# Spreading attention units over the stages of a fused attention and expert kernel: 12, 10, 8, 10, 5 in place of 10, 10, 10, 8, 7

## The chip, the cores and the metric

The kernel runs on one core of a Trainium2 chip. The metric is the device time of one execution in microseconds, the median of several runs. Before the change it is 318.38 us (three runs, 317.75 to 319.08). The profiled execution spans 316.5 us; the times of single instructions below are read in it, counted from its start.

## What is computed

Sliding-window attention with a distance bias, for 8 batches of 8 heads, 576 positions and 64 values per head, feeds an expert layer with 512 inputs, 2048 hidden values and 512 outputs per token. Inputs and output are float32.

```python
scores = (1.0 / np.sqrt(D)) * np.matmul(q, k.transpose(0, 1, 3, 2))
bias = slopes[:, None, None] * (-np.abs(rel))[None, :, :]
mask = (rel >= 0) & (rel < 128)
scores = np.where(mask, scores + bias[None], -1e9)
attn = softmax(scores)                       # over the last axis
x = np.matmul(attn, v).transpose(0, 2, 1, 3).reshape(B * S, H * D)
h = x @ w_in
g = h * np.cos(h)
out = g @ w_out
```

## The kernel before

The tokens, 4608 in all, pass through the expert layer in nine chunks of 512. Attention works in 72 units: for each batch eight units of a pair of heads and a half (256 queries), and a tail unit for the last 64 queries of all heads. Units are done in a fixed order, the first nine ahead of chunk 0, and the rest in stages: stage c stands between the first expert layer of chunk c and that of chunk c + 1, beside the second layer of chunk c. `QUOTA` says how many units each stage takes.

```python
QUOTA = [9, 9, 10, 10, 10, 8, 7]
...
def units(b):
    return [(b, pr, G) for G in range(2) for pr in range(NPAIR)] + [(b, "t", None)]
...
every = [u for b in range(B) for u in units(b)]
attention(every[0:9], -1)
done = 9
next_t = 2
for c in range(NCH):
    if c == 0:
        ...                                   # first layer of chunk 0, in halves
    else:
        for fc in range(NFC):
            moe1(c, fc, ...)                  # first layer, cosine, product
    n = QUOTA[c] if c < len(QUOTA) else 0
    attention(every[done:done + n], c)
    done += n
    while next_t < B and done >= 9 * (next_t - 1):
        load_v(next_t)
        if next_t < 4:
            tail_zero(next_t)
        dma_transposes(next_t)                # q and k of this batch, by SyncE's queue
        next_t += 1
        if next_t < B:
            load_nat("q", q, next_t)          # natural q, k, by GpSimd's queue
            load_nat("k", k, next_t)
    moe2(c)                                   # second layer
```

A stage's units go in groups of two. A group with a tail does its two value products one after the other. A finished unit has to be turned, from tokens along partitions to features along partitions. How this is done depends on when the next layer needs it: by DMA if the chunk of its first token is beyond the next stage's, and otherwise by TensorE with a copy by ScalarE or VectorE.

```python
def attention(us, phase):
    for g in range(0, len(us), 2):
        two = us[g:g + 2]
        ...                                   # scores, exponentials, masks
        for set_ in sets:
            pv(set_)                          # values
            after = []
            for u, ub in set_:
                n = ucount[0]
                ucount[0] += 1
                norm(u, ub, n)                # reciprocal and product, into xnat
                first = (S * u[0] + (512 if u[1] == "t" else 256 * u[2])) // CH
                after.append((first > phase + 1, u, ub, n))
            for by_dma, u, ub, n in after:
                if by_dma:
                    x_dma(u, n)
                else:
                    x_pe(u, ub, n)

def x_pe(u, ub, n):                           # two 128x128 transposes, then a copy
    ...
            for r in range(2):
                ins = e.transpose(dst[:, 128 * r:128 * r + 128],
                                  xnat[n % NX][:, 128 * r:128 * r + 128], ident[:, :])
    ...
    op(("act", "dve"), {"act": lambda e: e.activation(o, i, ACTF.Copy),
                        "dve": lambda e: e.tensor_copy(o, i)}, ...)

def x_dma(u, n):                              # one DMA transpose on SyncE's queue
    ...
    op("sp", [lambda e: e.dma_start_transpose(
        xT[:, pr, t0:t0 + 256].rearrange("p (r t) -> p r t", r=2), xnat[n % NX][:, :])], ...)
```

The order of instructions on each engine is not written by hand. The kernel records operations with their tiles, and a list scheduler with a model of durations, run when the kernel is built, places them: each engine takes the operation that can start soonest, by priority among those close together. GpSimd's operations keep the order in which they are recorded. ScalarE alternates between the exponential and the sine, stage by stage. SyncE's queue carries the transposes of q and k, the transposes of finished units and the stores of the output. The scores of batch b read buffers that batch b + 2 uses again, so a transpose of q or k waits for the last scores two batches before.

The second layer sums 16 matmuls per 128 tokens, the first layer four per 128 hidden values; both stream 512 columns per matmul.

Of the kernel before, what the change touches and what calls it, by code (L numbers as in the profile page):

```python
# [250 lines left out]
def bass_alibi_sliding__then__act_gcu_kernel(  # L251
# [8 lines left out]
    with ExitStack() as ctx:  # L260
# [31 lines left out]

        ps = ctx.enter_context(nc.psum_tensor("ps", [128, 8, 512], F32))
        BPE = 2
        QUOTA = [9, 9, 10, 10, 10, 8, 7]
        SB, UB, OB = [4, 5, 6, 7], [2, 3], [0, 1]

        slopes = [2.0 ** (-8.0 * (h + 1) / H) for h in range(H)]
# [487 lines left out]
# [4 lines that stand above are left out]
                if phase < 0:  # L790
                    for n, u in enumerate(two):
                        scores([u], n)
                        exps(u, n, 0)
                        mask(u)
                else:
                    scores(two, 0)
                    for n, u in enumerate(two):
                        exps(u, n, 2 * phase + 2)
                    for u in two:
                        mask(u)  # L800
                sets = [list(zip(two, OB if phase < 0 and g == 0 else UB))]
                if any(u[1] == "t" for u in two):
                    sets = [[s] for s in sets[0]]
                for set_ in sets:
                    pv(set_)
# [4 lines that stand above are left out]
                        norm(u, ub, n)  # L810
# [7 lines that stand above are left out]
# [27 lines left out]
        for c in range(NCH):  # L845
# [8 lines left out]
            else:  # L854
                for fc in range(NFC):
                    moe1(c, fc, (UB + SB)[fc % 6] if done < len(every) else
                         (UB + SB)[(16 * c + fc) % 6])
            n = QUOTA[c] if c < len(QUOTA) else 0
            attention(every[done:done + n], c)
# [40 lines left out]
```

The softmax here doesn't subtract the row's maximum and nothing guards it: scores larger than these inputs give would overflow.

## Time and profile before

| | before |
|---|---|
| median time | 318.38 us |
| span of the profiled execution | 316.5 us |
| matmuls on TensorE | 2480 |
| busy share of TensorE, ScalarE, VectorE, GpSimd | 96%, 66%, 60%, 30% |
| bytes moved by DMA | 37.63 MB |
| transposes of finished units by TensorE (line 661) | 80, for 40 units |
| DMA transposes of finished units (line 684) | 24 |

In the page's slices a digit is the busy share of one fortieth of the span (7.9 us), in tenths. A group's row gives the line, the engine, the operation, output and inputs, shape and count, then busy time, mean duration of one in ns and the idle time ahead of it. Durations of matmuls are modelled and overlap; the step from one start to the next tells what a matmul takes of TensorE. A timeline row has the start, the length, the engine, the line, the operation, its tiles and the count. A row of waits says who waited for whom, with the total in us, the number of times and the longest. "Landing" of a transfer is counted from its issue. Line 507 is scores, 498 scores of a tail, 592 and 595 values, 579 and 581 values of a tail, 697 the first layer, 768 the second, 742 the second layer's last tile; lines 372 and 375 are the DMA transposes of q and k (512 positions, then 64).

### The profile page before, as it was taken

Reading aid. Unit: us, or ns where it says so; the run is one execution under the profiler, and the core shown is the slowest. Engines: PE = TensorE matmul, PEld = TensorE weight load, DVE = VectorE, ACT = ScalarE, POOL = GpSimd, SP = SyncE. Lnnn points to the kernel's source line nnn. Section 1 sums busy time; section 2 is a strip of 40 time slices with the busy share of each in tenths; the row PEclk is TensorE's granted clock in tenths of the full one; section 3 lists DMA queues with packets and bytes.
Section 4 is the critical chain, followed back from the end, with each engine's and each line's share of the span. In section 5 each row is a group of like instructions: output and inputs, shape, how many; then the busy total and the mean of one; then the engine's idle time right before and its main releaser. Section 6 shows DMA issues by size and latency. Waiting matters only on the chain.

```text
span 316.5 us, 6268 instructions
## 1 busy us (share of the span) xinstructions
PE 304.9 (96%) x2480; PEld 155.9 (49%) x2480; DVE 188.5 (60%) x448; ACT 209.5 (66%) x306; POOL 95.1 (30%) x122
## 2 busy tenths in 40 slices
PE   2899999999999999999999999999999999999996
PEld 2677755444544544445444544544455444444444
DVE  3798757867685735848785878586555461363000
ACT  6896877886798746878687767857675553362211
POOL 8997140099946325701941300000000000000000
PEclk9999999999999999999999999999999999999999
DMA  7999999999999999999999894320012001201112
GB/s 139 178 207 208 206 164 186 142 139 190 140 131 173 174 151 203 156 142 132 150 165 143 112 143 77 106 68 18 25 74 47 33 0 48 87 0 68 66 72 94
DMA packets 142604, 37.63 MB, mean 119 GB/s; under 512 B 132208, under 2 KB 137328, under 8 KB 142576
## 3 DMA queue, kind: packets, MB, share of 16 engines
q0 software_dynamic: 99344, 18.10, 76.3%
q1 hardware_dynamic: 43232, 19.15, 31.9%
q8 instruction: 19, 0.31, 0.4%
q14 instruction: 9, 0.07, 0.1%
HBM read 36.70 MB, written 9.44 MB: 146 GB/s over the span
## 4 chain that ended last, share of the span: by engine, by line
PE 62%; DMA 18%; POOL 11%; SPq 6%; issue 1%; ACT 0%; POOLq 0%; ACTq 0%
PE ps L768 28%; PE ps L697 26%; DMA qnat<-in_q_dram 14%; SPq L372 6%; POOL vp L351 4%; POOL qnat L361 3%; PE ps L507 2%; DMA qt<-qnat 2%; DMA kt<-knat 2%; PE ps L592 2%; POOL knat L361 1%; PE ps L742 1%; POOL w_outb L389 1%; PE ps L595 1%; POOL w_inb L383 1%
## 5 line engine op out<-in xcount | busy, mean ns | idle before, releaser
L768 PE MATMUL ps<-w_outb,gT 128*128 128x512 bf16 x560 | 135.1, 379 | 0.0
L697 PE MATMUL ps<-xT,w_inb 128*128 128x512 bf16 x512 | 115.8, 379 | 0.0
L706 DVE TENSOR_TENSOR gT<-ps,cos 128x512 bf16<-128x512 f32 x128 | 81.9, 686 | 42.2 <-PE ps L768 29.8
L702 ACT ACTIVATE cos<-ps,halfpi 128x512 f32<-128x512 f32 x128 | 81.6, 688 | 29.2 <-PE ps L697 16.1
L768 PEld LDWEIGHTS ps<-w_outb,gT 128*128 128x128 bf16 x560 | 51.1, 98 | 54.7 <-issue 2.1
L697 PEld LDWEIGHTS ps<-xT,w_inb 128*128 128x128 bf16 x512 | 48.6, 98 | 57.5 <-DVE gT L706 4.0
L537 ACT ACTIVATE p<-ps 128x768 bf16<-128x768 f32 (+1 forms) x64 | 55.3, 915 | 15.4 <-PE ps L507 13.5
L351 POOL DMA_DIRECT2D vp<-in_v_dram x40 | 33.9, 890 | 58.1 <-PE ps L595 37.8
L561 DVE TENSOR_TENSOR p<-p,emask 128x512 bf16<-128x512 bf16 (+1 forms) x96 | 40.8, 461 | 14.9 <-ACT p L537 14.4
L774 ACT ACTIVATE ob<-ps 128x512 f32<-128x512 f32 x28 | 16.8, 599 | 41.8 <-PE ps L768 41.7
L361 POOL DMA_DIRECT2D qnat<-in_q_dram x30 | 25.6, 910 | 25.8 <-DMA qt<-qnat 18.4
L361 POOL DMA_DIRECT2D knat<-in_k_dram x30 | 25.6, 928 | 2.2 <-PE ps L720 2.2
L633 DVE TENSOR_TENSOR xnat<-ps,rec 128x256 bf16<-128x256 f32 x64 | 24.4, 420 | 0.3
L507 PE MATMUL ps<-qt,kt 64*128 64x128 bf16 (+1 forms) x320 | 19.1, 245 | 1.5 <-DVE kt L470 0.9
L592 PEld LDWEIGHTS ps<-vp,p 128*128 128x128 bf16 x256 | 15.5, 98 | 7.9 <-issue 4.3
L592 PE MATMUL ps<-vp,p 128*128 128x65 bf16 x256 | 18.3, 194 | 0.4 <-DVE p L561 0.2
L507 PEld LDWEIGHTS ps<-qt,kt 64*128 64x128 bf16 x320 | 11.4, 96 | 12.5 <-ACT p L537 4.0
L631 DVE RECIPROCAL rec<-ps 128x4 f32<-128x4 f32 x64 | 8.2, 167 | 15.5 <-PE ps L595 15.1
L595 PE MATMUL ps<-vp,p 128*128 128x65 bf16 x192 | 17.1, 193 | 0.0
L720 PE MATMUL ps<-xT,w_inb 128*128 128x256 bf16 x128 | 16.4, 273 | 0.2
L670 ACT ACTIVATE xT<-ps 128x256 bf16<-128x256 bf16 x27 | 9.9, 387 | 6.6 <-PE ps L661 6.5
L595 PEld LDWEIGHTS ps<-vp,p 128*128 128x128 bf16 x192 | 13.4, 97 | 0.4
(54 smaller groups left out, 174.6 us busy)
## 6 DMA issues: line engine op xcount, KB each, us to landing
out_dram<-ob SPq DMA_DIRECT2D x35, 256.0 KB, 2.3
vp<-in_v_dram POOLq DMA_DIRECT2D x32, 128.0 KB, 11.3
qnat<-in_q_dram POOLq DMA_DIRECT2D x24, 128.0 KB, 12.4
knat<-in_k_dram POOLq DMA_DIRECT2D x24, 128.0 KB, 15.7
w_inb<-in_moe_w_in_dram POOLq DMA_DIRECT2D x4, 512.0 KB, 10.7
w_outb<-in_moe_w_out_dram POOLq DMA_DIRECT2D x4, 512.0 KB, 22.5
qrows<-in_q_dram POOLq DMA_DIRECT2D x1, 576.0 KB, 15.4
krows<-in_k_dram POOLq DMA_DIRECT2D x1, 576.0 KB, 17.5
```

The costliest lines, as they stand in the source:

```text
L351: op("pool", [lambda e, t=t, rows=rows: e.dma_start(vp[b % 2][0:rows, t, :, 0:64], v[b, :, 128 * t:128 * t + rows, :].rearrange("h p d -> ...
L361: fns.append(lambda e, t=t, rows=rows: e.dma_start(nat[which][b % 2][0:rows, t, :, :], src[b, :, 128 * t:128 * t + rows, :].rearrange("h p ...
L507: ins = e.matmul(ps[:, banks[x], c0:c1], keys_ap(b, x, pr, kc), query_ap(b, x, pr, qb, 128 * nb), start=True, stop=True)
L537: op("act", lambda e: e.activation(P[i][:, :, 0:hi], src_[:, :, 0:hi], ACTF.Exp, scale=0.125), w=held + [("P", i)], occ=920 if G else 691, ...
L561: op("dve", lambda e, p=p, m=m: e.tensor_tensor(p, p, m, ALU.mult), r=[("P", i), ("EM", h0), ("EM", h1)], w=[("P", i)] if n != 1 else [("P ...
L592: ins = e.matmul(o, P[i][:, x, d0:d0 + 128], V[:, kc, h, 0:65], start=True, stop=not two)
L595: ins = e.matmul(o, P[i][:, x, p0:p0 + 128], V[:, kc - 1, h, 0:65], start=False, stop=True)
L633: op("dve", lambda e: e.tensor_tensor(o, U[:, :, :, 0:64], rv[:, :, :, None].broadcast_to([128, 2, 2, 64]), ALU.mult), r=[("rec", n % 2)], ...
L697: op("pe", lambda e, kc=kc: e.matmul(ps[:, bank, :], w_in[:, kc, 128 * fc:128 * fc + 128], xT[:, kc, r0:r0 + CH], start=(kc == 0), stop=(k ...
L702: op("act", lambda e: e.activation(cosb[ci][:, :], ps[:, bank, :], ACTF.Sin, bias=halfpi[:, 0:1]), r=["halfpi"], w=[("B", bank), ("cos", c ...
L706: op("dve", lambda e: e.tensor_tensor(gT[gi][:, fc, :], ps[:, bank, :], cosb[ci][:, :], ALU.mult), r=[("cos", ci)], w=[("B", bank), ("g", ...
L768: op("pe", lambda e, t=t, fc=fc, bank=bank: e.matmul(ps[:, bank, :], gT[gi][:, fc, 128 * t:128 * t + 128], w_out[:, fc, :], start=(fc == 0 ...
```

## The change

Five numbers of `QUOTA` change, of which one (10 units in stage 3) comes out the same. Two units move from stage 3's start to stage 2's end, two from stage 4 to stage 3, and two from stage 6 to stage 5. The numbers of instructions of attention and of the expert layers stay, as do thresholds, buffers and priorities; how a unit is turned follows from the rule above, and the scheduler lays out anew what comes after. Its purpose is a distribution of attention work over the stages that the schedule's model, in which DMA engines are shared between the queues, finds shorter. The other items that the change is named after (the first q piece by SyncE's queue, a block of w_in ahead of the rest of V, doubled natural q and k tiles) are in the kernel before already.

```diff
         BPE = 2
-        QUOTA = [9, 9, 10, 10, 10, 8, 7]
+        QUOTA = [9, 9, 12, 10, 8, 10, 5]
         SB, UB, OB = [4, 5, 6, 7], [2, 3], [0, 1]
```

## The prediction

> **What bounds the kernel now.** I read four views of the profile of before, from the coarse to the fine. First the page: the busy line, the slices and the two costliest groups.
>
> ```profile
> PE 304.9 (96%) x2480; PEld 155.9 (49%) x2480; DVE 188.5 (60%) x448; ACT 209.5 (66%) x306; POOL 95.1 (30%) x122
> ...
> PE   2899999999999999999999999999999999999996
> ...
> DMA  7999999999999999999999894320012001201112
> ...
> L768 PE MATMUL ps<-w_outb,gT 128*128 128x512 bf16 x560 | 135.1, 379 | 0.0
> L697 PE MATMUL ps<-xT,w_inb 128*128 128x512 bf16 x512 | 115.8, 379 | 0.0
> ```
>
> TensorE is at 9 tenths in every slice but the first two and the last. The 379 ns of a matmul is a modelled, pipelined time and does not add up (1072 of 379 ns would be 406 us), so a busy PE row does not yet prove that PE is the bound. What proves it is start to start: in the timeline near the end 48 matmuls stand between 299.82 and 310.18, so one takes 10.36/48 = 0.216 us, and the stretches inside attention keep the same pace. Second view, TensorE's waits from 118 us to the end, which is where the change acts:
>
> ```profile
> PE ps L498 <- DMA kt<-knat: 0.6, 1, 0.6
> ```
>
> That is the whole answer. In 198 us TensorE has one visible wait, 0.6 us, for the key transpose of batch 4. Third, the chain that ended last: from that wait on it is TensorE's own instructions, back to back, except for the closing copy of ScalarE.
>
> ```profile
> 112.00 6.59 DMA kt<-knat
> 118.58 0.05 issue
> 118.63 0.41 PE ps L498 x16
> 119.04 0.17 PE ps L507 x4
> 119.20 1.40 PE ps L768 x6
> ```
>
> So before 118.6 us the chain goes through DMA (18% of the span), and after it time can fall only if TensorE has fewer instructions, or cheaper changes between kinds. It can rise by any new wait. ScalarE (66%) and VectorE (60%) are not the bound in the mean; the DMA engines are at 9 tenths until about 190 us, so what needs a transfer there can be late.
>
> **What the Trainium skill says.** *Perfetto Trace Analysis*, section "Identifying the Most-Contended Engine", says that matmul busy time is no good measure of closeness to the roofline; this trace agrees (379 ns shown, 0.216 us start to start), so I count starts. *TensorE: Matmul & The Clock Gate*, section "Wait — 56ns, not 53.3ns?", gives 215.7 ns per 512 columns at the full clock; the trace has 0.216 us, and the PEclk row is at 9 or more throughout, so I see no slack in the matmuls themselves. *DMA: Bandwidth & Descriptors*, section "Issuing engines are not separate DMA queues", says that transfers of SyncE and GpSimd share the same 16 engines and interleave. That bears on the DMA transposes that the change adds; the trace shows such transfers landing 2.3 to 6.5 us after their issue, longest while GpSimd's loads run.
>
> **The change part by part.** The same 72 units are done in the same order. Only the stage that does a unit changes: after the first 9, stages 0 to 6 take 9, 9, 12, 10, 8, 10, 5 in place of 9, 9, 10, 10, 10, 8, 7. Finished units after stages 2 to 6 are 39, 49, 57, 67, 72 in place of 37, 47, 57, 65, 72. The loads of batches 4 to 7 are placed by thresholds of 27, 36, 45 and 54 finished units; these fall in the same stages, and GpSimd's instructions keep their order exactly. TensorE's order is the same up to the wait at 118.63 us. So I start there.
>
> *Removed.* A unit whose tokens are needed by the very next stage is turned by TensorE (two 128x128 transposes and a copy); one needed later is turned by DMA. By the rule in the kernel 40 units go by TensorE before: 3, 2, 1 and 2 of them in stages 3, 4, 5, 6. After, it is 1, 0, 1 and 0: 34 in all. Thus 6 pairs of transposes and 6 copies (384 ns on ScalarE or 284 on VectorE, off the path) go. What a pair costs TensorE, from the timeline:
>
> ```profile
> 171.73 1.03 PE L768 MATMUL ps<-w_outb,gT 128*128 128x512 bf16 x4
> 172.64 0.28 PE L661 MATMUL ps<-ident,xnat 128*128 128x128 bf16 x2
> 172.76 0.38 PE L768 MATMUL ps<-w_outb,gT 128*128 128x512 bf16 x1
> ```
>
> The pair takes 172.76 - 172.64 = 0.12 us; the four matmuls before it take 0.91 us where 4 x 0.216 = 0.86 are due. Over the eight such pairs after 118.6 us I find 0.119 us, and 0.030 us more in the matmuls ahead. So 6 x 0.149 = **0.9 us** less on the path. TensorE's order in the changed program also has 14 passages from second-layer matmuls to scores instead of 16; in the trace such a passage costs 0.10 us beyond the matmul pace, so **0.2 us** more. Score, value and expert matmuls keep their numbers.
>
> *Added.* Six DMA transposes of 128x256, 24 becoming 30. Each holds SyncE's queue 1.2 us. They are needed a stage or more later, so their landing is not on the path; what stands behind them in the queue may be. *Moved.* Two units of batch 4 go from stage 3 to stage 2, two of batch 5 from 4 to 3, two of batch 7 from 6 to 5. TensorE moves them bodily: 1.3 to 1.4 us for two, paid in one stage and saved in a later one, so zero in the sum. Sum: 0.9 + 0.2 = 1.1 us. Laying the whole changed order out from 118.63, each stretch at its mean in the trace, gives 1.3 us; the 0.2 us between are small waits that the trace's passages contain, of which I keep half: **1.2 us saved** if no wait is added.
>
> **The rivals.** *First, a later key transpose.* Batch 6's keys wait in SyncE's queue behind the column transposes of stage 3:
>
> ```profile
> 157.20 2.54 SPq L684 DMA_TRANSPOSE xT<-xnat  x2
> 159.78 5.25 SPq L372 DMA_TRANSPOSE kt<-knat  x1
> 165.08 1.25 SPq L375 DMA_TRANSPOSE kt<-knat  x1
> ```
>
> The second of these was issued at 165.08 and landed 6.4 us on, at 171.5. After, two more column transposes stand ahead (four in place of two): 2 x 1.25 = 2.5 us, so 174.0. The first scores of batch 6 share a group with batch 5's tail, which TensorE started at 176.48. In the changed order the work from 118.63 to that group is 3 second-layer matmuls more (0.65 us) and 4 pairs of transposes less (0.6 us), so it is due at 176.5 again. The margin goes from 5.0 to 2.5 us. If landing drifts by over 2.5 us, TensorE waits; at worst I give it 2 us. *Batch 4's keys*: the wait at 118.63 has the same 13 matmuls ahead of it, so 0.6 us again. Batch 5's keys landed at 134.78 + 7.7 = 142.5 and are wanted at 149.3 by my count (149.0 before); batch 7's at 197.16 + 2.9 = 200.1 against 206.5 (206.9 before).
>
> *Second, ScalarE and VectorE as the bound of an attention stretch.* In stage 2 the extra pair's scores would be issued near 121.6, two exponentials of 0.81 us end near 123.8, VectorE's masks near 124.5, and TensorE's order puts the values at about 124.7. That is tight: 0 to 0.3 us of wait there, and the same at the ends of stages 3 and 5, each of which has a further group with four to eleven matmuls as cover. Against a larger loss: every stage keeps its one table load for the exponential and one for the sine (1283 ns each, 7 and 7), and ScalarE waits for TensorE in the first layer, not the reverse. Together I set 0.2 us for new waits.
>
> *Third, a real gain from filling the late stages.* If TensorE starved in stage 5 or 6, spreading units would help by several us. The single visible wait after 118 us speaks against it: nothing can be filled that is already full.
>
> **Range and chances.** 318.4 - 1.2 + 0.2 = 317.4. Times of before spread over 317.75 to 319.08, so the range must hold about 0.7 us of noise each way, plus a possible 1 us of new waits: **316.3 to 318.8**. Two per cent would be 6.4 us; no step reaches a third of it. Chances: faster 0.01, within 2% 0.98, slower 0.01.
>
> **What would show each step.** In the profile after: 68 transposes of line 661 instead of 80 and 30 column transposes on SyncE; TensorE's 2480 matmuls 2468; the waits of TensorE after 118 us again little more than the one of 0.6 us; the last stretch of second-layer matmuls (started at 310.2 by the last tile) about 1 us earlier; the first scores of batch 6 near 176.5 with their keys landed near 174. I am wrong upward if a key transpose appears as TensorE's releaser with over 1 us, or if waits for exponentials or masks appear at the ends of stages 2, 3 or 5; wrong downward if the wait at 118.6 goes, which would give 0.6 us.

## The result, and the profile after

The changed kernel took 317.38 us (median of six runs, 317.06 to 317.82) against 318.39 us for the kernel before in the same comparison: a ratio of 0.9966, with a 95% interval of 0.9950 to 0.9982. That is about 1.0 us less, and in the range. (Four entries of `QUOTA` differ, not five as the section on the change has it.) Where the microsecond comes from is another matter, and most of what follows is about that.

The page of the changed kernel, with the rows that answer to those shown of before:

```profile
PE 304.4 (96%) x2468; PEld 155.6 (49%) x2468; DVE 188.9 (60%) x447; ACT 207.1 (66%) x301; POOL 95.1 (30%) x122
...
PE   2799999999999999999999999999999999999996
...
DMA  7999999999999999999999694222013001201112
...
L768 PE MATMUL ps<-w_outb,gT 128*128 128x512 bf16 x560 | 134.0, 380 | 0.0
L697 PE MATMUL ps<-xT,w_inb 128*128 128x512 bf16 x512 | 115.0, 379 | 0.1
```

TensorE has the 12 matmuls fewer that were foretold (2468), and is as full as before. ScalarE and VectorE together have six instructions fewer. The span is 315.7 us in place of 316.5.

The span hides two parts that have to be read apart. They meet where TensorE starts the tail scores of batch 3, the group that has to wait for batch 4's keys. Up to there TensorE's order is the same in both kernels. From there to the last tile of the second layer lies all that the change touches on TensorE. The timeline of TensorE in the kernel before has these two marks:

```profile
118.63 0.41 PE L498 MATMUL ps<-qt,kt 64*128 64x64 bf16 x16 [0.65 <-DMA kt<-knat]
...
310.18 3.66 PE L742 MATMUL ps<-w_outb,gT 128*128 128x256 bf16 x32
```

The same in the changed kernel:

```profile
118.15 0.41 PE L498 MATMUL ps<-qt,kt 64*128 64x64 bf16 x16
...
309.37 3.66 PE L742 MATMUL ps<-w_outb,gT 128*128 128x256 bf16 x32
```

The second part takes 310.18 - 118.63 = 191.55 us before and 309.37 - 118.15 = 191.22 us after: only **0.33 us** less. The other 0.48 us of the marks' shift came earlier: the wait of 0.65 us for batch 4's keys is absent in this profile of the changed kernel. I call the second part "the part after the keys" below.

### The profile page after: what moved, and what is told of

The parts are those of the page before. It is cut to its first block, busy times and chain, and to the rows that moved or that the text cites. A ratio compares the mean times of both kernels' runs of the same rounds, so it can differ in the third digit from the quotient of the medians.

```text
span 315.7 us, 6247 instructions
## 1 busy us (share of the span) xinstructions
PE 304.4 (96%) x2468; PEld 155.6 (49%) x2468; DVE 188.9 (60%) x447; ACT 207.1 (66%) x301; POOL 95.1 (30%) x122
## 4 chain that ended last, share of the span: by engine, by line
PE 91%; DMA 6%; DVE 1%; POOL 0%; issue 0%; ACT 0%; ACTq 0%
PE ps L768 39%; PE ps L697 35%; DMA qrows<-in_q_dram 5%; PE ps L507 5%; PE ps L592 3%; PE ps L720 2%; PE ps L454 2%; PE ps L595 2%; DMA ob<-in_q_dram 1%; PE ps L661 1%; PE ps L742 1%; PE ps L579 1%; PE ps L498 1%; PE ps L581 1%; POOL w_inb L383 0%; DVE gT L706 0%
## 5 line engine op out<-in xcount | busy, mean ns | idle before, releaser
L774 ACT ACTIVATE ob<-ps 128x512 f32<-128x512 f32 x26 | 15.5, 598 | 40.7 <-PE ps L768 40.6
L776 DVE COPY ob<-ps 128x512 f32<-128x512 f32 x9 | 6.2, 690 | 13.6 <-PE ps L768 13.6
```

## Experiments

Theory A is the prediction's: a pair of TensorE transposes less is 0.15 us less, because TensorE is full. Rival B: the profile's gain is mostly the chance of when batch 4's keys land. Rival C: placing the units elsewhere saves the time, and the transposes were hidden. Runs named e1 to e4 were compared with the kernel before on one chip (median 317.94 us), e5 to e7 on another (318.00), e8 apart (317.86); so runs of different groups are compared by their ratios, which are not quite the quotients of the medians.

| run | median us | ratio to before (95% interval) | part after the keys, us | against before's 191.55 |
|---|---|---|---|---|
| e1: changed kernel again | 317.41 | 0.9979 (0.9965 to 0.9993) | 191.23 | -0.32 |
| e2: units moved, turned by TensorE | 317.82 | 0.9992 (0.9979 to 1.0006) | 191.39 | -0.16 |
| e3: units not moved, turned by DMA | 316.86 | 0.9964 (0.9948 to 0.9979) | 190.79 | -0.76 |
| e4: all units but the tails turned by TensorE | 321.11 | 1.0089 (1.0061 to 1.0116) | 194.76 | +3.21 |
| e5: kernel before again | 318.19 | 1.0008 (0.9996 to 1.0020) | 191.56 | +0.01 |
| e6: moved, stages 3 to 6 all by DMA | 316.89 | 0.9964 (0.9951 to 0.9978) | 190.67 | -0.88 |
| e7: not moved, stages 3 to 6 all by DMA | 316.59 | 0.9957 (0.9941 to 0.9972) | 190.58 | -0.97 |
| e8: not moved, stages 2 to 6 all by DMA | 318.84 | 1.0024 (1.0010 to 1.0038) | - | - |

**e1, the changed kernel again.** No edit.

> The changed kernel once more, for the spread. Theory A (six pairs of TensorE transposes less, each about 0.15 us on the path): about 1.0 us under before (317.4), and the part of the trace after the wait for batch 4's keys shorter by 0.3 to 1.0 us. Rival B (the earlier landing of batch 4's keys, 117.3 against 118.6 us, in a stretch where both kernels have the same order, was chance and gave most of the 0.8 us of the profile): the landing falls back to about 118.6 and the time lies 0.3 to 0.5 us under before.

Its gain came out smaller, 0.9979. Its profile spans 317.0 us, longer than before's 316.5. The cause stands in TensorE's waits after 100 us:

```profile
PE ps L498 <- DMA kt<-knat: 1.4, 1, 1.4
```

The same instructions waited 1.4 us here and not at all in the first profile, while the part after the keys is 191.23 us against 191.22. So rival B holds for a single profile, though not just as written: the landing did not fall back to 118.6, it went to 119.4. Theory A's 0.3 to 1.0 us for the part is met only at its lower edge.

**e2, the units moved but still turned by TensorE.**

```diff
-                        after.append((first > phase + 1, u, ub, n))
+                        after.append((first > phase + 1 and u not in
+                            {(4, 1, 0), (4, 2, 0), (5, 2, 0), (5, 3, 0), (7, 2, 0), (7, 3, 0)},
+                            u, ub, n))
```

> The changed distribution (12, 10, 8, 10, 5), but the six units that it hands to DMA stay with TensorE: 80 transposes of line 661 again. Theory A: most of the gain is gone, 0.0 to 0.5 us under before (318.0 to 318.4; laying out its order from before's stretches gives 0.45 under, for fewer passages). Rival C (the placing of the units saves the time, the transposes are hidden): 1.0 us under before, 317.4.

The ratio's interval holds 1, and the part is 0.16 us shorter. Rival C, which wanted 317.4, falls: moving the units is worth next to nothing.

**e3, the old distribution, with the six units turned by DMA.**

```diff
-                        after.append((first > phase + 1, u, ub, n))
+                        after.append((first > phase + 1 or u in
+                            {(4, 1, 0), (4, 2, 0), (5, 2, 0), (5, 3, 0), (7, 2, 0), (7, 3, 0)},
+                            u, ub, n))
```

> The old distribution (10, 10, 10, 8, 7), but the six units are turned by DMA: 68 transposes of line 661, 30 of line 684. Theory A: 1.0 us under before (317.4), as the changed kernel, if the DMA transposes land before the first layer of the next chunk wants them (they have about 8 us). Rival C: as before, 318.4.

This has the gain without the change: 0.9964, and 0.76 us in the part, more than twice the 0.33 us of the changed kernel. Its two marks are:

```profile
117.89 0.41 PE L498 MATMUL ps<-qt,kt 64*128 64x64 bf16 x16
...
308.68 3.66 PE L742 MATMUL ps<-w_outb,gT 128*128 128x256 bf16 x32
```

A turn by DMA takes away a copy as well as a pair of transposes, and no run parts the two. The starts do: the transposes of line 661 take 0.24 us of this part in place of 0.95, which is 0.71 of the 0.76 us. So the transposes are what counts, and the new distribution gives part of them back.

**e4, the dose the other way: 24 pairs more.**

```diff
-                        after.append((first > phase + 1, u, ub, n))
+                        after.append((first > phase + 1 and u[1] == "t", u, ub, n))
```

> The old distribution, every unit but the tails turned by TensorE: 24 pairs more, 128 transposes of line 661, none of line 684. Theory A: 24 x 0.15 = 3.6 us over before, 321.7 to 322.0. Rival C: hidden, under 1 us over before. If ScalarE's and VectorE's copies begin to count, over 4 us.

The median rose by 3.2 us (2.8 us by the ratio, whose interval allows 1.9 to 3.7), and the part by 3.21 us: 3.21/24 = 0.134 us for a pair. Theory A has the mechanism; its 0.149 us is somewhat too much. No jump shows that copies on ScalarE or VectorE begin to count.

**e5, the kernel before again.** No edit.

> The kernel before once more, timed against itself: a ratio of 1.000, and what its interval leaves open. In the trace the part from the wait for batch 4's keys to the last tile is 191.55 us again (theory A: that part repeats, the changed kernel's two profiles have 191.22 twice); the wait itself may be anything from 0 to 1.5 us (rival B), and its spread bounds what one profile can say of the rest.

The part repeats to 0.01 us, 191.56. Two profiles of before and two of the changed kernel thus agree within 0.01 us there, and 0.33 us is a clear difference. The ratio 1.0008 tells how far a comparison of a kernel with itself strays.

**e6, the changed distribution, the last two TensorE pairs of stages 3 to 6 also by DMA; e7, the same rule in the old distribution.** Both kernels have this edit:

```diff
-                        after.append((first > phase + 1, u, ub, n))
+                        after.append((first > phase + 1 or phase > 2, u, ub, n))
```

> The changed distribution, and in stages 3 to 6 the two units that TensorE still turns go by DMA as well: 64 transposes of line 661. Theory A: 2 x 0.14 us less than the changed kernel, the part after the wait about 190.9 in place of 191.22, time 0.3 us under the changed kernel. If the waits for masks and for a free bank take it back: 191.2 again.

> The old distribution, and every unit of stages 3 to 6 turned by DMA: 8 pairs less than before, 64 transposes of line 661, 32 DMA transposes of line 684. Theory A: 8 x 0.13 = 1.05 us under before, the part after the wait about 190.5 (190.79 with six of them). Rival C: no better than before. If DMA turns too late for the next chunk: a wait of the first layer for DMA at a stage's end, over 0.3 us.

In e7 eight pairs less are 0.97 us less, 0.121 us each, a little under the 1.05 us expected. It has the lowest median and the shortest part of all, with the old `QUOTA`; the intervals of its ratio and of those of e3 and e6 overlap. In e6 two pairs less than the changed kernel saved 0.55 us of the part, twice the expected 0.3; a wait of 0.29 us that is shown below for the changed kernel is gone there. The list of TensorE's waits after 100 us is empty in both profiles, and no start of the first layer is late after the second: every turn by DMA landed in time.

**e8, stage 2 by DMA too.** The edit is that of e7 with `phase > 1`.

> The old distribution, every unit of stages 2 to 6 turned by DMA: 8 pairs of TensorE transposes less than in the kernel that does so from stage 3 on (48 transposes of line 661). If each pair were worth 0.13 us wherever it stands: 1.0 us less again, 315.6. If a turn by DMA is free only with time to land: SyncE's queue takes eight column transposes of 1.25 us behind batch 4's keys (112 us), so the last lands near 129 us, while the first layer of chunk 3 is due at 120 to 124: a wait of 3 to 8 us of TensorE for DMA in stage 2, and 319 to 324 us.

Eight pairs less again, and yet the ratio is 1.0024 where e7 has 0.9957; its runs spread from 317.11 to 320.34 us. (The eight pairs stood ahead of the mark, so the part after the keys tells nothing here.) In its profile SyncE's queue reaches stage 2's turns only behind batch 4's keys, and TensorE waits. First SyncE, then TensorE, then the weight loads that go ahead of TensorE's matmuls, in their timelines:

```profile
110.36 1.88 SPq L375 DMA_TRANSPOSE kt<-knat  x1
112.28 3.85 SPq L684 DMA_TRANSPOSE xT<-xnat  x3
116.24 0.52 SPq L780 DMA_DIRECT2D out_dram<-ob  x1
116.81 7.27 SPq L684 DMA_TRANSPOSE xT<-xnat  x5
...
125.94 5.72 PE L697 MATMUL ps<-xT,w_inb 128*128 128x512 bf16 x24 [0.99 <-issue]
...
125.91 0.56 PEld L697 LDWEIGHTS ps<-xT,w_inb 128*128 128x128 bf16 x4 [1.46 <-issue]
126.92 1.41 PEld L697 LDWEIGHTS ps<-xT,w_inb 128*128 128x128 bf16 x8 [0.46 <-DMA xT<-xnat]
128.89 1.19 PEld L697 LDWEIGHTS ps<-xT,w_inb 128*128 128x128 bf16 x7 [0.56 <-DMA xT<-xnat]
```

The first layer stands still for 0.99 us before its start at 125.94. The row names no releaser, but one of these transfers landed at 125.85, just ahead of it. The two later weight loads name the transfers themselves; by TensorE's starts they cost another 0.13 and 0.23 us. The last three transfers landed 5.6 to 7.4 us after their issue. The wait is smaller than the 3 to 8 us expected, and the median a little under the 319 to 324 us: the scheduler put 22 second-layer matmuls between the tail scores of batch 3 and the first layer, where e7 has 6. This profile lacks some matmul records, and its execution took 317.81 us where the median is 318.84, so it need not show the whole loss.

## Why the prediction was right, and where its sum was not

The time, the range and the mechanism held. The pieces of the 1.2 us did not, and errors of both signs met. That the measured 1.0 us is the foretold 1.0 us is in part luck: the part that the change touches gave 0.33 us.

*The transposes.* Predicted 0.149 us for a pair, 0.9 us for six. From the starts in the changed kernel's trace the pairs after the keys take 0.25 us in place of 0.95, and the matmuls ahead of them hold 0.10 us less: **0.8 us** in all. (Of the 0.24 us ahead of all eight pairs, the two that stay hold 0.14.) The mechanism and nearly the size stand. But a pair is not worth 0.149 us in the end. Net of everything it was 0.121 (e7), 0.127 (e3: 0.76/6) and 0.134 us (e4). In e7 and e3 the waits ahead of values grow, from 1.05 us before to 1.33 and 1.19; the likely reason, which no run isolates, is that TensorE, having less to do, comes earlier to the masks. In e4 they hardly change (1.09 us); there an added pair holds up the matmul ahead of it by only 0.013 us in place of 0.030.

*The passages.* Predicted 0.2 us for two passages from second-layer matmuls to scores that vanish. They did not vanish, they changed partner. In the changed kernel two score groups follow a tail's values directly; TensorE's timeline has:

```profile
208.79 0.19 PE L579 MATMUL ps<-vp,ptail 128*128 128x65 bf16 x1
208.81 0.19 PE L581 MATMUL ps<-vp,ptail 128*128 128x65 bf16 x1
208.94 0.50 PE L507 MATMUL ps<-qt,kt 64*128 64x256 bf16 x8
```

The value matmuls start 0.03 us apart, and the scores 0.125 us after the last of them: the same 0.095 us extra that a passage from the second layer costs. Eighteen passages into scores stand before and after. This term is **zero**. The 0.45 us expected of e2 leaned on the same fewer passages; its part was 0.16 us shorter, of which 0.09 us are shorter waits ahead of values.

*New waits.* Predicted 0.2 us. The clearest is one that I had not named. After stage 6 TensorE fills six PSUM banks with first-layer matmuls of chunk 7 and must then have one emptied. In the changed kernel VectorE and TensorE show this:

```profile
246.02 3.68 DVE L706 TENSOR_TENSOR gT<-ps,cos 128x512 bf16<-128x512 f32 x6 [5.15 <-PE ps L768]
...
242.59 4.05 PE L768 MATMUL ps<-w_outb,gT 128*128 128x512 bf16 x18
246.77 1.04 PE L697 MATMUL ps<-xT,w_inb 128*128 128x512 bf16 x4
```

The 18 matmuls should take 18 x 0.216 = 3.89 us and the next start at 246.48; it starts at 246.77, **0.29 us** late. VectorE's product had waited 5.15 us for second-layer matmuls: chunk 7 writes the `gT` buffer that chunk 5's second layer still reads. The product starts at 246.02, takes 0.69 us, and its bank is free at 246.7. Before, the corresponding rows are:

```profile
246.78 3.68 DVE L706 TENSOR_TENSOR gT<-ps,cos 128x512 bf16<-128x512 f32 x6 [3.93 <-PE ps L768]
...
244.35 3.40 PE L768 MATMUL ps<-w_outb,gT 128*128 128x512 bf16 x15
247.59 1.67 PE L697 MATMUL ps<-xT,w_inb 128*128 128x512 bf16 x7
```

The same 24 first-layer matmuls stand ahead, but TensorE was busy to 247.59, long enough to cover the product. That another `gT` buffer would end the wait is not shown by any run. The list of TensorE's waits does not show the 0.29 us, because a matmul's modelled 379 ns end covers it; only starts do. (The weight loads show it: those of line 697 wait 0.6 us for this product, 0.3 us before.) The waits ahead of values sum to 1.24 us in the changed kernel against 1.05 us before, **0.2 us** more, as had been allowed.

*The sum.* 0.8 us for transposes, less 0.2 us ahead of values and 0.3 us for a bank: 0.3 us, as the part's 0.33 us shows. I foretold 1.0 us: the passages (0.2), the small waits (0.1) and the bank (0.3) are the difference.

*Batch 4's keys.* "0.6 us again" was the step that failed for a single run: 0.65, 0.54, 0, 1.4 us in the four profiles of before, before, changed, changed. This wait supplied the other half of the first profile's gain; the prediction had named its going as the sign of being wrong downward, worth 0.6 us. Without it the account closes nearly: the lowest times in the comparison of e1 to e4 are 317.42 us for before, 317.08 for the changed kernel (0.34 less), 317.33 for e2 (0.09 less), 316.55 for e3 (0.87 less) and 320.64 for e4 (3.22 more), in each case within 0.11 us of the part after the keys. The medians put the changed kernel 0.5 to 1.0 us below before. Why its typical run lies nearer to its lowest one than before's does is left open: the runs without a profile do not show their waits. Nor is it shown that the landing is chance alone: in seven of the eight profiles that are not of before, batch 4's keys landed at 116.9 to 117.7 us, in both of before at 118.4 to 118.6, and e1 shows that the changed kernel too can have them at 119.4.

*Batch 6's keys.* I set 174.0 us for their landing, by adding 2.5 us of queue. SyncE's queue in the changed kernel:

```profile
156.79 5.07 SPq L684 DMA_TRANSPOSE xT<-xnat  x4
161.91 5.95 SPq L372 DMA_TRANSPOSE kt<-knat  x1
167.91 1.24 SPq L375 DMA_TRANSPOSE kt<-knat  x1
```

The issue moved as reckoned, from 165.08 to 167.91, but the transfer landed 4.1 us on in place of 6.4, at 172.0. In e1 it landed at 175.3, with TensorE there at 177.5. So the margin of 2.5 us that I gave was about right at its least, and no wait arose; a landing is not the issue plus a constant. The rival of a starved late stage, worth several us, is refuted by e2: moving the units alone changes nothing that the timing resolves.

## What to carry to other kernels

Where an engine is full, count what it no longer has to do, then look for the waits that the new order brings; another distribution over stages that were full already was worth nothing here that the timing resolves (e2). Split a trace at the last point up to which both kernels have the same order: the part after it repeated to 0.01 us in two profiles of before and two of the changed kernel, while a DMA landing ahead of it moved one profile by 1.3 us against another of the same kernel. If the gain comes from a side effect of a rule (here which engine turns a unit), change the rule: e7 has a greater gain with the old schedule, and e8 shows that the gain ends where the transfer no longer has time to land.

## What I had not expected of the hardware

A change into scores costs TensorE 0.095 us whatever stood before it, a 512-column or a 65-column matmul; in e4 it is the same after a 128-column transpose. Scores use 64 rows, their neighbours 128; that this is the reason is not shown. And the landing of DMA transposes under load spreads widely between profiles with unchanged code: batch 4's keys landed at 118.6 and 118.4 us in the two profiles of before, at 117.3 and 119.4 in those of the changed kernel.
